# Attention and GeGLU on one core: the order of two exps in shared steps, and the planner's table of engine times

## The chip, the core and the metric

The kernel runs on one NeuronCore of a Trainium2 chip. The metric is device time in microseconds (us) of one execution; each kernel is run several times and the median counts. The profile shows one execution, taken by the hardware profiler. Four engines matter here: TensorE (PE in the profile, with its weight loads as PEld), ScalarE (ACT), VectorE (DVE) and GpSimd (POOL). SyncE (SP) only issues DMAs.

## The reference

A pre-norm transformer block over 2048 tokens of width 640, with 32 query heads of width 20 that share one key and one value head, and a GeGLU feed-forward layer of width 1536. Everything is bfloat16 outside the accumulations. Cut to its core:

```
xn = (x - mean(x)) / sqrt(var(x) + 1e-5)
q = xn @ wq  -> 32 heads x 20;   k = xn @ wk;   v = xn @ wv        # one k, one v
p = softmax(q k^T / sqrt(20))                                       # 32 x 2048 x 2048
h = x + concat(p v) @ wo
hn = layernorm(h)
out = h + (gelu(hn @ w_gate) * (hn @ w_up)) @ w_down                # gelu in its tanh form
```

The softmax needs 32 x 2048 x 2048 = 134 million exponentials, which is where most of the time goes.

## The kernel before

**Tiling.** The 2048 tokens are 16 tiles of 128 (NT). For each tile of queries the heads are taken in two halves, and for each half the 16 tiles of keys are gone through one after the other. One such combination is a *step*; there are NS = 512 of them, 32 to a tile. A step computes four scores matmuls (L729) that use four row strips of the PE array at once, each a 128x512 block: 128 keys by 4 heads x 128 queries. Each fills one bank of the scores memory (PSUM).

**Banks.** Of the eight banks six form three pairs (A_BANKS, pool pA). A step takes two pairs, `t1` and `t2`. So the next step finds one pair left over from the step before this one, and has to wait until this step gives back its first pair. One more bank collects the weighted sum of values (V_BANKS), one serves all projections (M_BANKS).

**The exps.** In a plain step ACT takes the exp of both pairs, each in one instruction over 1024 columns (`exp2`, L745, tile `pa_sb`): a *pair exp*. In a *shared* step ACT does one pair exp and, of the other pair, one bank (`exp1`, L754, tile `ps_sb`): a *half-bank exp*. The second bank of that pair is done by DVE with integer arithmetic on the bits of a bfloat16 (`exp_dve`): `e1` (L768, tile `ej`) reads the bank and so frees it, and for each two such banks four more instructions over 1024 columns finish the exp: `e2` (L779, tile `eu`), `e3` (L781, tile `et`), `e4` (L782, tile `et`), `e5` (L783, tile `pd_sb`). The pair is given back when both the half-bank exp and e1 have read it (`t2.n_rel = 2`).

**The rest.** Four matmuls per step multiply the exps with the values (PV, L840, `v_ext`). Every 16 steps the sums are evacuated, their reciprocals taken through a small trip to HBM and back, and multiplied in on POOL. Every 32 steps a tile goes through the output projection (L917), a layer norm on DVE, a transposing DMA, and the feed-forward matmuls (L992, L1031), which are cut into chunks and laid between the steps of later tiles; so are the query projections (L632). DVE evacuates their results.

**What sets the order.** A planner in the kernel, run while the program is built, writes out the order of each engine's queue. It simulates the five engines with a table of times: each `Op` has a duration on its engine, and `SEEN[engine]` is added before a result counts as visible to the one that waits for it. An engine takes, among the operations that can start first, the one of lowest `prio`; exps and e1 have -1000. `urgent` keeps PE from beginning a chunk that would hold up the next scores matmuls. Whether a step is shared is decided when its scores have been placed (`scored`): it is, if the work that DVE still has to do adds up to less than `D_BACKLOG` = 800 ns. Each engine gets its queue in the order written, with waits on semaphores where an input comes from elsewhere.

Of the kernel before, what the change touches and what calls it, by code (L numbers as in the profile page):

```python
# [8 lines left out]
ALU = mybir.AluOpType  # L9
# [8 lines left out]
SEEN = {"pe": 120.0, "act": 60.0, "dve": 50.0, "pool": 60.0, "sp": 0.0}  # L18
DRAIN = 107.0
SP_ISSUE = 550.0  # L20

# [43 lines left out]
class Planner:  # L65
# [107 lines left out]
    def run(self):  # L173
        while True:
            best = None
            for e in ENGINES:
# [21 lines left out]
                if best is None or first < best[0]:  # L198
                    if e == "pe":
                        u = self.urgent(first)  # L200
                        if u is not None:
                            ok = [(a, op) for a, op in tl if op.prio <= -1000 or
                                  a + op.dur + (DRAIN if op.mode != self.pe_mode else 0.0) <= u or a >= u]
                            if not ok:
                                continue
                            tl = ok
                            first = min(a for a, _ in tl)
                            if best is not None and first >= best[0]:
                                continue
                    pick = min((op.prio, a, k) for k, (a, op) in enumerate(tl) if a <= first + 1e-6)  # L210
                    best = (first, e, tl[pick[2]][1])
# [103 lines left out]
def bass_sequential_preLN__grouped_kv_mqa__glu_gated_geglu__prompt_kernel(  # L315
# [26 lines left out]
    D_FROM, D_BACKLOG, SLACK = 14, 800.0, 100.0  # L342
    MLAG, DLAG, VLAG, VLATE = 300.0, 100.0, 400.0, 1200.0
# [106 lines left out]
    def dve(fn, n, deps, prio, mode=1.04, fix=150.0, **kw):  # L450
        return op("dve", fn, fix + n * mode, deps, prio, **kw)
# [8 lines left out]
    def evac(eng, o_ap, i_ap, n, deps, prio, **kw):  # L460
        return op(eng, copy_fn(o_ap, i_ap), (220 + .833 * n) if eng == "act" else (150 + 1.04 * n), deps, prio, **kw)
# [47 lines left out]
    def ln(which, t0, n, src, prio, gate=None, free=None, tmode="dma"):  # L509
# [3 lines left out]
        for t in range(t0, t0 + n):  # L513
            for hf in range(2):
                st.append(dve((lambda t, hf: lambda e: e.bn_stats(
                    stats[:, L, t, 6 * hf:6 * hf + 6], xh[:, t, hf * hq:(hf + 1) * hq]))(t, hf),
                    hq, (src(t),), prio, fix=130, gate=gate, name=f"st{L}.{t}"))
        ag = []
        for t in range(t0, t0 + n):
            ag.append(dve((lambda t: lambda e: e.bn_aggr(mv[:, L, t, :], stats[:, L, t, :]))(t), 12,  # L520
                          st[2 * (t - t0):2 * (t - t0) + 2], prio, fix=195, name=f"ag{L}.{t}"))
        a = dve(lambda e: e.tensor_copy(mvb[:, L, sl, :], mv[:, L, sl, :]), 2 * n, ag, prio, fix=165)
        b = dve(lambda e: e.tensor_copy(mvf[:, L, sl, :], mvb[:, L, sl, :]), 2 * n, (a,), prio, fix=165)
        c = dve(lambda e: e.tensor_scalar_add(veb[:, L, sl], mvf[:, L, sl, 1], EPS), n, (b,), prio, fix=170)
        d = op("pool", lambda e: e.tensor_tensor(den[:, L, sl], veb[:, L, sl], halfc[:, 0:n], ALU.pow),
               230 + 170 * n, (c, m_half), prio - 50)
        r = dve(lambda e: e.reciprocal(rsd[:, L, sl], den[:, L, sl]), n, (d,), prio, fix=175)
        res = []
        for t in range(t0, t0 + n):
# [3 lines left out]
                D, (r, b, src(t)), prio, mode=.26, fix=220, acq=[tl], name=f"nm{L}.{t}")  # L533
# [226 lines left out]
    def exp_dve(o_, tile):  # L760


        if dstate["tile"] is None:
# [6 lines left out]
            690, (o_,), prio=-1000, acq=[jt] if k == 0 else [], name="e1"))  # L770
        pl.rel(tile, p1)
        firsts.append(p1)
        if k == 0:
            fin = Op("dve", None, 690, (), prio=-950, acq=[pt], name="e5", late=VLATE)
            dstate["fin"] = fin
        fin = dstate["fin"]
        if k == 1:
            ut, wt = Tile(pU), Tile(pW)
            e2 = pl.add(Op("dve", lambda e: e.tensor_scalar(eu[:], ej[:, jt.slot, :], 127, None, ALU.bitwise_and),  # L779
                           430, firsts, prio=-950, acq=[ut], name="e2"))  # L780
            e3 = pl.add(Op("dve", lambda e: e.tensor_scalar(et[:], eu[:], C2, C1, ALU.mult, ALU.add), 430, (e2,), prio=-950, acq=[wt], name="e3"))  # L781
            e4 = pl.add(Op("dve", lambda e: e.tensor_tensor(et[:], et[:], eu[:], ALU.mult), 690, (e3, e2), prio=-950, name="e4"))  # L782
# [20 lines left out]
    def scored(s, o_, t1, t2):  # L803
# [144 lines left out]
    def ln2(t, r1, r2, prio):  # L948
# [3 lines left out]
        s0 = dve(lambda e: e.bn_stats(stats[:, L, t, 0:6], xh[:, t, 0:hq]), hq, (r1,), p, fix=130)  # L952
        s1 = dve(lambda e: e.bn_stats(stats[:, L, t, 6:12], xh[:, t, hq:D]), hq, (r1, r2), p, fix=130)
        ag = dve(lambda e: e.bn_aggr(mv[:, L, t, :], stats[:, L, t, :]), 12, (s0, s1), p, fix=195)
        a = dve(lambda e: e.tensor_copy(mvb[:, L, sl, :], mv[:, L, sl, :]), 2, (ag,), p, fix=165)
        b = dve(lambda e: e.tensor_copy(mvf[:, L, sl, :], mvb[:, L, sl, :]), 2, (a,), p, fix=165)
        c = dve(lambda e: e.tensor_scalar_add(veb[:, L, sl], mvf[:, L, sl, 1], EPS), 1, (b,), p, fix=170)
        d = op("pool", lambda e: e.tensor_tensor(den[:, L, sl], veb[:, L, sl], halfc[:, 0:1], ALU.pow),
               400, (c, m_half), p - 50)
        r = dve(lambda e: e.reciprocal(rsd[:, L, sl], den[:, L, sl]), 1, (d,), p, fix=175)  # L960
# [3 lines left out]
            D, (r, b, r1, r2), p, mode=.26, fix=220, acq=[tl])  # L964
# [164 lines left out]
```

## Time and profile before

| | |
|---|---|
| median of 3 runs | 1015.47 us (1013.6 to 1015.71) |
| profiled execution | 1015.34 us, of it span of the instructions 1013.6 us |
| ACT busy | 887.5 us (88%) |
| DVE busy | 735.9 us (73%) |
| PE busy | 705.4 us (70%) |
| mean granted clock of PE | 0.853 |
| first pair exp to last pair exp | about 20 us to 981 us |
| pair exps, half-bank exps | 708, 316 |

Busy time is the sum of what the profile shows as the duration of instructions. Instructions of one engine can overlap at their ends, so three pair exps in a row take less than three durations; the distance from start to start is what the engine's queue goes by. A row of the timeline merges equal neighbours: "x3" is three instructions, and the time beside it runs from the start of the first to the end of the last. The number in brackets is how long the engine was idle before, and what ended that. PEclk is the share of its full clock that PE was granted; the records have it at 1.00 or 0.50, and means lie between.

### The profile page before, as it was taken

The numbers are of one execution on the slowest core, as the hardware profiler recorded it, in microseconds if no ns is written. First come the engines' busy times: TensorE is split into PE (matmuls) and PEld (weight loads), VectorE is DVE, ScalarE is ACT, GpSimd is POOL, SyncE is SP. The second block draws the span as 40 slices with busy tenths as digits, with TensorE's granted clock in tenths as the row PEclk, the third lists the DMA queues.
The fourth block names the chain that finished last, engine by engine and source line by source line (L and its number), as shares of the span: only waits on it lengthen the run. The fifth ranks groups of instructions, "written<-read, shape, count | busy, mean of one in ns | idle before, by whom it ended". The sixth has DMA issues, their size and how long they took to land.

```text
span 1013.6 us, 15962 instructions
## 1 busy us (share of the span) xinstructions
PE 705.4 (70%) x6313; PEld 276.9 (27%) x6313; DVE 735.9 (73%) x1447; ACT 887.5 (88%) x1056; POOL 66.9 (7%) x70
## 2 busy tenths in 40 slices
PE   2665756777777667667677676767777676777687
PEld 2321111232223222233222331223222222212245
DVE  8457677787878777876787676876788766778654
ACT  2698888899899999999999998999989999989971
POOL 5000000010001000000000000000000000000000
PEclk9776665798789998998898987988979888869899
DMA  6750000000000000000000000000000000000010
GB/s 171 124 209 12 12 18 12 8 22 8 12 25 19 12 18 16 17 12 12 19 25 18 4 16 12 25 19 12 15 11 18 18 12 19 19 14 20 7 22 21
DMA packets 47282, 27.42 MB, mean 27 GB/s; under 512 B 34408, under 2 KB 41960, under 8 KB 47208
## 3 DMA queue, kind: packets, MB, share of 16 engines
q1 hardware_dynamic: 47208, 26.40, 10.3%
q8 instruction: 50, 0.82, 0.3%
q14 instruction: 24, 0.20, 0.1%
HBM read 18.34 MB, written 2.88 MB: 21 GB/s over the span
## 4 chain that ended last, share of the span: by engine, by line
ACT 53%; PE 28%; DVE 11%; issue 5%; DMA 2%; POOL 0%; SPq 0%; POOLq 0%
ACT pa_sb L745 47%; PE ps L729 14%; PE ps L992 5%; DVE ej L768 4%; PE ps L840 4%; ACT ps_sb L754 3%; PE ps L1031 2%; ACT gh L1010 2%; PE ps L632 2%; DVE eu L779 1%; DVE et L781 1%; PE ps L917 1%; DMA xnT<-xn 1%; ACT L745 1%; ACT L1010 1%
## 5 line engine op out<-in xcount | busy, mean ns | idle before, releaser
L745 ACT ACTIVATE pa_sb<-ps 128x1024 bf16<-128x1024 f32 x708 | 685.5, 1032 | 83.5 <-PE ps L729 66.3
L729 PE MATMUL ps<-qT,kT 32*128 32x512 bf16 x2048 | 233.7, 443 | 265.9 <-ACT pa_sb L745 212.8
L768 DVE TENSOR_SCALAR ej<-ps 128x512 uint16<-128x512 f32 x316 | 218.1, 690 | 174.2 <-PE ps L729 172.4
L754 ACT ACTIVATE ps_sb<-ps 128x512 bf16<-128x512 f32 x316 | 190.3, 602 | 0.8 <-PE ps L729 0.8
L729 PEld LDWEIGHTS ps<-qT,kT 32*128 32x128 bf16 x2048 | 59.9, 93 | 473.4 <-ACT pa_sb L745 201.4
L840 PE MATMUL ps<-pa_sb,v_ext 128*32 128x512 bf16 x1416 | 176.6, 436 | 4.2 <-ACT pa_sb L745 3.3
L840 PE MATMUL ps<-ps_sb,v_ext 128*32 128x512 bf16 x316 | 116.3, 443 | 0.0
L840 PE MATMUL ps<-pd_sb,v_ext 128*32 128x512 bf16 x316 | 116.3, 443 | 0.0
L782 DVE TENSOR_TENSOR et<-et,eu 128x1024 bf16<-128x1024 bf16 x158 | 111.2, 704 | 2.2
L783 DVE TENSOR_TENSOR pd_sb<-ej,et 128x1024 uint16<-128x1024 uint16 x158 | 107.9, 683 | 0.9
L890 POOL TENSOR_TENSOR onT<-osb,rL 128x512 bf16<-128x512 f32 x31 | 40.5, 1305 | 628.3 <-DMA rL<-lscr 628.3
L992 PE MATMUL ps<-xnT,wu 128*128 128x256 bf16 (+1 forms) x540 | 74.8, 286 | 8.2 <-ACT gh L1010 8.2
L1031 PE MATMUL ps<-wd,gh 128*128 128x128 bf16 (+1 forms) x384 | 74.3, 326 | 1.4 <-DVE gh L1015 0.7
L781 DVE TENSOR_SCALAR et<-eu 128x1024 bf16<-128x1024 uint16 x158 | 72.4, 458 | 2.3
L992 PE MATMUL ps<-xnT,wg 128*128 128x256 bf16 (+1 forms) x540 | 72.0, 276 | 0.4 <-DVE gh L457 0.4
L779 DVE TENSOR_SCALAR eu<-ej 128x1024 uint16<-128x1024 uint16 x158 | 67.8, 429 | 2.3
L840 PEld LDWEIGHTS ps<-pa_sb,v_ext 128*32 128x32 bf16 x1416 | 41.0, 100 | 88.8 <-issue 55.7
L992 PEld LDWEIGHTS ps<-xnT,wu 128*128 128x128 bf16 x540 | 46.2, 104 | 35.4 <-issue 16.0
L917 PE MATMUL ps<-wo_pad,onT 128*128 128x512 bf16 (+1 forms) x256 | 50.8, 330 | 2.6 <-DVE onT L874 1.1
L992 PEld LDWEIGHTS ps<-xnT,wg 128*128 128x128 bf16 x540 | 45.2, 102 | 25.3 <-issue 14.2
L1015 DVE TENSOR_TENSOR gh<-gh,ps 128x512 bf16<-128x512 bf16 x48 | 32.8, 686 | 20.9 <-PE ps L992 20.4
L632 PE MATMUL ps<-xnT,wq_pad 128*128 128x256 bf16 x280 | 47.3, 309 | 0.0
(68 smaller groups left out, 416.8 us busy)
## 6 DMA issues: line engine op xcount, KB each, us to landing
rL<-lscr SPq DMA_DIRECT2D x124, 64.0 KB, 2.0
out_dram<-xh SPq DMA_DIRECT2D x16, 160.0 KB, 1.8
lcol<-osb SPq DMA_DIRECT2D x124, 2.0 KB, 1.7
xh<-in_A_x_dram SPq DMA_DIRECT2D x6, 320.0 KB, 6.8
wg<-in_B_w_gate_dram SPq DMA_DIRECT2D x1, 1920.0 KB, 8.2
wu<-in_B_w_up_dram SPq DMA_DIRECT2D x1, 1920.0 KB, 12.5
wd<-in_B_w_down_dram SPq DMA_DIRECT2D x1, 1920.0 KB, 17.3
gh<-in_A_wq_dram SPq DMA_DIRECT2D x2, 400.0 KB, 4.6
```

The lines of the kernel that those rows point to most:

```text
L632: ins = e.matmul(tbank(mt)[:, i * 256:(i + 1) * 256], wq_pad[:, c, g, :], xnT[:, c, tok], start=(c == 0), stop=(c == ND - 1))
L729: ins = e.matmul(bank(A_BANKS[(t1, t1, t2, t2)[r].slot] + r % 2), kT4[32 * r:32 * r + 32, kt * P:(kt + 1) * P], qT[32 * r:32 * r + 32, (t ...
L745: ex = pl.add(Op("act", lambda e: e.activation(pa_sb[:, pt.slot, :], bank(A_BANKS[tile.slot], 2), ACT.Exp, scale=SM), 928, (o_,), prio=-10 ...
L754: ex = pl.add(Op("act", lambda e: e.activation(ps_sb[:, pt.slot, :], bank(A_BANKS[tile.slot]), ACT.Exp, scale=SM), 502, (o_,), prio=-1000, ...
L768: p1 = pl.add(Op("dve", lambda e: e.tensor_scalar(ej[:, jt.slot, k * 512:(k + 1) * 512], bank(A_BANKS[tile.slot] + 1), EA, EB, ALU.mult, A ...
L779: e2 = pl.add(Op("dve", lambda e: e.tensor_scalar(eu[:], ej[:, jt.slot, :], 127, None, ALU.bitwise_and), 430, firsts, prio=-950, acq=[ut], ...
L781: e3 = pl.add(Op("dve", lambda e: e.tensor_scalar(et[:], eu[:], C2, C1, ALU.mult, ALU.add), 430, (e2,), prio=-950, acq=[wt], name="e3"))
L782: e4 = pl.add(Op("dve", lambda e: e.tensor_tensor(et[:], et[:], eu[:], ALU.mult), 690, (e3, e2), prio=-950, name="e4"))
L783: fin.fn = lambda e: e.tensor_tensor(pd_sb[:, pt.slot, :], ej[:, jt.slot, :], et[:], ALU.add)
L840: ins = e.matmul(bank(V_BANKS[vt.slot])[32 * r:32 * r + 32, :], v_ext[:, kt, :], us[r][2](), start=(kt == 0), stop=(kt == NKT - 1), tile_p ...
L992: ins = e.matmul(tbank(m)[:, j * n:(j + 1) * n], w[:, c, fc * P:(fc + 1) * P], xnT[:, c, tok], start=(c == 0), stop=(c == ND - 1))
L1031: ins = e.matmul(tbank(tl_)[:, 0:c1 - c0], H(f // nfu, f // nfu + 1)[:, (f % nfu) * n + i * P:(f % nfu) * n + (i + 1) * P], wd[:, f, c0:c1 ...
```

## The change

It has three parts.

1. In a shared step the pair that ACT and DVE share can now be `t1`, with its half-bank exp (and e1) first and the pair exp second. That is done when DVE, by the plan, is free no later than 150 ns (`D_EARLY`) after the scores are seen; else the order is as before.
2. The planner's table of times is split in two: an operation's duration is now the distance after which its engine can start the next one, and the rest until a result is seen is in `SEEN` (by another engine) and `SELF` (by the same engine). Durations of DVE instructions fall, most of them by 70 to 90 ns, `SEEN` rises from 60 to 220 ns for ACT and from 50 to 190 ns for DVE.
3. DVE may be kept free: if an e1 can start within 300 ns (`HOLD`), only operations that end before it are placed ahead of it.

```diff
-SEEN = {"pe": 120.0, "act": 60.0, "dve": 50.0, "pool": 60.0, "sp": 0.0}
+SEEN = {"pe": 120.0, "act": 220.0, "dve": 190.0, "pool": 150.0, "sp": 0.0}
+SELF = {"pe": 0.0, "act": 150.0, "dve": 115.0, "pool": 80.0, "sp": 0.0}
+HOLD = 300.0
...
         if d.eng == op.eng:
-            return d.end + SEEN[d.eng]
+            return d.end + SELF[d.eng]
...
-                    pick = min((op.prio, a, k) for k, (a, op) in enumerate(tl) if a <= first + 1e-6)
-                    best = (first, e, tl[pick[2]][1])
+                    lim = first + 1e-6
+                    if e == "dve":
+                        soon = [a for a, op in tl if op.prio <= -1000 and a <= first + HOLD]
+                        if soon:
+                            lim = min(soon) + 1e-6
+                            tl = [(a, op) for a, op in tl if a > first + 1e-6 or op.prio <= -1000 or a + op.dur <= lim]
+                            lim = max(lim if all(a > first + 1e-6 for a, op in tl if op.prio > -1000) else first + 1e-6, min(a for a, _ in tl))
+                    pick = min((op.prio, a, k) for k, (a, op) in enumerate(tl) if a <= lim)
+                    best = (max(first, tl[pick[2]][0]), e, tl[pick[2]][1])
...
-    def dve(fn, n, deps, prio, mode=1.04, fix=150.0, **kw):
+    def dve(fn, n, deps, prio, mode=1.04, fix=72.0, **kw):
...
             ej[:, jt.slot, k * 512:(k + 1) * 512], bank(A_BANKS[tile.slot] + 1), EA, EB, ALU.mult, ALU.add),
-            690, (o_,), prio=-1000, acq=[jt] if k == 0 else [], name="e1"))
+            610, (o_,), prio=-1000, acq=[jt] if k == 0 else [], name="e1"))
...
-        us = exp2(o_, t1)
         use_d = dstate["tile"] is not None or (D_FROM <= s < NS - 6 and dve_backlog(o_.end) < D_BACKLOG)
         if use_d:
-            t2.n_rel = 2
-            us.append(exp1(o_, t2))
-            us.append(exp_dve(o_, t2))
-            state["nd"] = state.get("nd", 0) + 1
+            first = pl.free["dve"] < o_.end + SEEN["pe"] + D_EARLY
+            ta, td = (t2, t1) if first else (t1, t2)
+            td.n_rel = 2
+            if first:
+                us = [exp1(o_, td), exp_dve(o_, td)]
+                us += exp2(o_, ta)
+            else:
+                us = exp2(o_, ta)
+                us += [exp1(o_, td), exp_dve(o_, td)]
         else:
-            us += exp2(o_, t2)
+            us = exp2(o_, t1) + exp2(o_, t2)
```

The other lines of the diff are durations of the same kind (e2 and e3 from 430 to 345, e4 and e5 from 690 to 610, and the small instructions of the layer norms).

**What it does to the queues.** In the program that is built, 334 of 340 shared steps have the half-bank exp first. There were 316 shared steps; there are now 340, so 684 pair exps in place of 708, and 12 more groups e1, e1, e2 to e5 on DVE. Two places show how the queues changed. The rows give line, instruction, tiles, size, and the semaphore waited for (s_pe is PE's, s_dve DVE's own).

ACT's queue in the first tile, a few shared steps after sharing begins. Before:

```order
L754 ACTIVATE ps_sb<-ps 128x512
L745 ACTIVATE pa_sb<-ps 128x1024 [waits s_pe]
L754 ACTIVATE ps_sb<-ps 128x512
L745 ACTIVATE pa_sb<-ps 128x1024 [waits s_pe]
L754 ACTIVATE ps_sb<-ps 128x512
L745 ACTIVATE pa_sb<-ps 128x1024 [waits s_pe]
L745 ACTIVATE pa_sb<-ps 128x1024
```

Now:

```order
L756 ACTIVATE pa_sb<-ps 128x1024
L765 ACTIVATE ps_sb<-ps 128x512 [waits s_pe]
L756 ACTIVATE pa_sb<-ps 128x1024
L765 ACTIVATE ps_sb<-ps 128x512 [waits s_pe]
L756 ACTIVATE pa_sb<-ps 128x1024
L756 ACTIVATE pa_sb<-ps 128x1024 [waits s_pe]
L756 ACTIVATE pa_sb<-ps 128x1024
```

The wait for the step's scores has moved from the pair exp to the half-bank exp: instructions still alternate, but a shared step now begins with the short one and ends with the long one.

DVE's queue at the first four shared steps (`ej` is e1, `eu` e2, `et<-eu` e3, `et<-et,eu` e4, `pd_sb` e5, `qT` the evacuation of a query projection). Before:

```order
L768 TENSOR_SCALAR ej<-ps 128x512 [waits s_pe]
L457 CAST qT<-ps 128x512 [waits s_pe]
L768 TENSOR_SCALAR ej<-ps 128x512 [waits s_pe]
L782 TENSOR_TENSOR et<-et,eu 128x1024 [waits s_dve]
L779 TENSOR_SCALAR eu<-ej 128x1024 [waits s_dve]
L783 TENSOR_TENSOR pd_sb<-ej,et 128x1024
L768 TENSOR_SCALAR ej<-ps 128x512 [waits s_dve,s_pe]
```

Now:

```order
L779 TENSOR_SCALAR ej<-ps 128x512 [waits s_pe]
L468 CAST qT<-ps 128x512 [waits s_pe]
L779 TENSOR_SCALAR ej<-ps 128x512 [waits s_pe]
L793 TENSOR_TENSOR et<-et,eu 128x1024
L794 TENSOR_TENSOR pd_sb<-ej,et 128x1024 [waits s_dve]
L790 TENSOR_SCALAR eu<-ej 128x1024
L792 TENSOR_SCALAR et<-eu 128x1024 [waits s_dve]
L793 TENSOR_TENSOR et<-et,eu 128x1024 [waits s_dve]
L779 TENSOR_SCALAR ej<-ps 128x512 [waits s_pe]
```

Between the fourth and the fifth e1 stand now five instructions in place of three: e5 of the first group directly after its e4, and most of the second group.

More of the change, by code (lines that the diff above doesn't have):

```diff
@@ L342, in bass_sequential_preLN__grouped_kv_mqa__glu_gated_geglu__prompt_kernel @@
     D_FROM, D_BACKLOG, SLACK = 14, 800.0, 100.0
+    D_EARLY = 150.0
     MLAG, DLAG, VLAG, VLATE = 300.0, 100.0, 400.0, 1200.0
@@ L516, in ln @@
                     stats[:, L, t, 6 * hf:6 * hf + 6], xh[:, t, hf * hq:(hf + 1) * hq]))(t, hf),
-                    hq, (src(t),), prio, fix=130, gate=gate, name=f"st{L}.{t}"))
+                    hq, (src(t),), prio, fix=60, gate=gate, name=f"st{L}.{t}"))
         ag = []
@@ L773, in exp_dve @@
         if k == 0:
-            fin = Op("dve", None, 690, (), prio=-950, acq=[pt], name="e5", late=VLATE)
+            fin = Op("dve", None, 610, (), prio=-950, acq=[pt], name="e5", late=VLATE)
             dstate["fin"] = fin
@@ L779, in exp_dve @@
             e2 = pl.add(Op("dve", lambda e: e.tensor_scalar(eu[:], ej[:, jt.slot, :], 127, None, ALU.bitwise_and),
-                           430, firsts, prio=-950, acq=[ut], name="e2"))
-            e3 = pl.add(Op("dve", lambda e: e.tensor_scalar(et[:], eu[:], C2, C1, ALU.mult, ALU.add), 430, (e2,), prio=-950, acq=[wt], name="e3"))
-            e4 = pl.add(Op("dve", lambda e: e.tensor_tensor(et[:], et[:], eu[:], ALU.mult), 690, (e3, e2), prio=-950, name="e4"))
+                           345, firsts, prio=-950, acq=[ut], name="e2"))
+            e3 = pl.add(Op("dve", lambda e: e.tensor_scalar(et[:], eu[:], C2, C1, ALU.mult, ALU.add), 345, (e2,), prio=-950, acq=[wt], name="e3"))
+            e4 = pl.add(Op("dve", lambda e: e.tensor_tensor(et[:], et[:], eu[:], ALU.mult), 610, (e3, e2), prio=-950, name="e4"))
             fin.fn = lambda e: e.tensor_tensor(pd_sb[:, pt.slot, :], ej[:, jt.slot, :], et[:], ALU.add)
@@ L963, in ln2 @@
             xn[:, tl.slot, :], xh[:, t, :], mvf[:, L, t, 0:1], rsd[:, L, t:t + 1], ALU.subtract, ALU.mult),
-            D, (r, b, r1, r2), p, mode=.26, fix=220, acq=[tl])
+            D, (r, b, r1, r2), p, mode=.26, fix=190, acq=[tl])
         return [(nm, tl)]
```

28 lines of the change are left out of this document (14 added, 14 removed).

## The prediction

> **What bounds the kernel now.** The page comes first: its shares and its costliest groups.
>
> ```profile
> span 1013.6 us, 15962 instructions
> PE 705.4 (70%) x6313; PEld 276.9 (27%) x6313; DVE 735.9 (73%) x1447; ACT 887.5 (88%) x1056; POOL 66.9 (7%) x70
> ...
> ACT 53%; PE 28%; DVE 11%; issue 5%; DMA 2%; POOL 0%; SPq 0%; POOLq 0%
> ...
> L745 ACT ACTIVATE pa_sb<-ps 128x1024 bf16<-128x1024 f32 x708 | 685.5, 1032 | 83.5 <-PE ps L729 66.3
> ...
> L768 DVE TENSOR_SCALAR ej<-ps 128x512 uint16<-128x512 f32 x316 | 218.1, 690 | 174.2 <-PE ps L729 172.4
> L754 ACT ACTIVATE ps_sb<-ps 128x512 bf16<-128x512 f32 x316 | 190.3, 602 | 0.8 <-PE ps L729 0.8
> ```
>
> ACT is the busiest engine, and it idles before pair exps, waiting for scores (PE, L729). The half-bank exps hardly wait: each follows a pair exp of its own step. So the stall falls once per step, before the pair exp that opens it. To see its size I went to the timeline, first where PE had its full clock (508.3 to 528.7 us, row further down):
>
> ```profile
> 508.93 2.85 ACT L745 ACTIVATE pa_sb<-ps 128x1024 bf16<-128x1024 f32 x3 [0.60 <-PE ps L729]
> ...
> 512.28 1.02 ACT L745 ACTIVATE pa_sb<-ps 128x1024 bf16<-128x1024 f32 x1
> 512.28 0.69 DVE L768 TENSOR_SCALAR ej<-ps 128x512 uint16<-128x512 f32 x1 [0.44 <-PE ps L729]
> 513.21 0.59 ACT L754 ACTIVATE ps_sb<-ps 128x512 bf16<-128x512 f32 x1
> 513.45 0.40 PE L729 MATMUL ps<-qT,kT 32*128 32x512 bf16 x4 [0.68 <-ACT pa_sb L745]
> 513.90 2.85 ACT L745 ACTIVATE pa_sb<-ps 128x1024 bf16<-128x1024 f32 x3
> ...
> 524.06 1.02 ACT L745 ACTIVATE pa_sb<-ps 128x1024 bf16<-128x1024 f32 x1
> 525.67 1.02 ACT L745 ACTIVATE pa_sb<-ps 128x1024 bf16<-128x1024 f32 x1
> 527.28 1.02 ACT L745 ACTIVATE pa_sb<-ps 128x1024 bf16<-128x1024 f32 x1
> 528.89 1.94 ACT L745 ACTIVATE pa_sb<-ps 128x1024 bf16<-128x1024 f32 x2
> ```
>
> Read it as a loop. The pair exp runs 512.28 to 513.30; only then is a bank pair free, and the next scores start at 513.45 (0.15 later), take 0.40, and the next exp starts at 513.90 (0.05 later). 1.02 + 0.15 + 0.40 + 0.05 = 1.62 us, which is the distance 512.28 to 513.90. The next shared steps take 1.61 each (524.06, 525.67, 527.28, 528.89). ACT itself needs less: three pair exps in 2.85 us start (2.85 - 1.02) / 2 = 0.915 apart, so 0.10 of an exp's duration lies under the next; a half-bank exp then takes 0.602 - 0.11 = 0.49. Together 1.41. A shared step loses 0.20 us, because the short exp does not cover the scores.
>
> The same at half clock:
>
> ```profile
> 502.62 1.02 ACT L745 ACTIVATE pa_sb<-ps 128x1024 bf16<-128x1024 f32 x1 [0.23 <-PE ps L729]
> 503.79 0.62 PE L729 MATMUL ps<-qT,kT 32*128 32x512 bf16 x4 [0.25 <-ACT pa_sb L745]
> 504.33 1.89 PE L1031 MATMUL ps<-wd,gh 128*128 128x512 bf16 x4
> 504.45 1.02 ACT L745 ACTIVATE pa_sb<-ps 128x1024 bf16<-128x1024 f32 x1 [0.32 <-PE ps L729]
> 506.82 1.02 ACT L745 ACTIVATE pa_sb<-ps 128x1024 bf16<-128x1024 f32 x1 [0.86 <-PE ps L729]
> 506.82 0.69 DVE L768 TENSOR_SCALAR ej<-ps 128x512 uint16<-128x512 f32 x1 [1.34 <-PE ps L729]
> ```
>
> The scores take 0.62 and the loop is 1.83. The step from 504.45 takes 2.37: there PE is held by four matmuls of the feed-forward layer (1.89 us), which no order of exps changes.
>
> How many steps are of which kind comes from the windows view for L754 (columns: stretch, length, busy with count, PEclk), and four stretches of all engines:
>
> ```profile
> 52.00:201.00 149.00, 32.26 (x54) 0.66 0.13 42
> 201.00:960.00 759.00, 156.20 (x259) 0.88 0.06 16
> ...
> 498.00:508.20 10.20, 7.23 (x42) 1.47 (x42) 8.34 (x14) 8.47 (x12) 1.05 (x1) 0.50 0.01 2
> 508.30:528.70 20.40, 14.67 (x150) 5.14 (x146) 16.83 (x31) 19.37 (x25) 1.27 (x1) 1.00 0.07 23
> ...
> 617.60:627.70 10.10, 7.13 (x42) 1.48 (x42) 7.30 (x13) 8.37 (x12) 0.09 (x1) 0.50 0.01 2
> 627.80:648.00 20.20, 14.47 (x153) 5.05 (x146) 16.69 (x30) 19.23 (x25) 1.39 (x1) 1.00 0.10 23
> ```
>
> A mean clock c between 0.5 and 1 means a share of 2 x (1 - c) at half clock: 68% of the first stretch, 24% of the second. So 0.68 x 54 + 0.24 x 259 = 99 shared steps ran at half clock, 217 at full clock.
>
> **The change part by part.** *Half-bank exp first.* The next scores now wait for the half-bank exp (0.60) and e1 (0.69), both started by the same scores. The trace has no scores released by an e1 alone; the nearest row is the 0.15 behind the pair exp, and I take it. From e1's start: 0.69 + 0.15 + 0.40 + 0.05 = 1.29 us to the next exp at full clock. Meanwhile ACT is busy for 0.49 + 0.915 = 1.41 us, so the scores are hidden and ACT sets the pace, with 0.12 to spare. At half clock the loop is 0.69 + 0.15 + 0.62 + 0.05 = 1.51, still 0.10 over ACT's time. The price that the trace does not show is how late e1 starts: below zero it can't go; from above, it can stand behind one DVE instruction of 0.69 that has just started. In the rows above e1 starts with the pair exp (512.28, 506.82). I add 0.02: 1.43 and 1.52.
>
> At full clock, 1.60 now (1.62, 1.61, 1.61, 1.61 above, and the step before 512.28, which is 508.93 + 2 x 0.915 = 510.76 to 512.28, 1.52): 217 x (1.60 - 1.43) = 37 us. The bounds are 217 x 0.19 = 41 us and, with each e1 a whole instruction late, a loss (below). At half clock I take three steps in four as free of a blocking chunk: the steps of 616.81 to 626.42 below take 1.84, 1.74 (from 618.65 + 2 x 0.915 = 620.48), 1.83 and 2.37. The three average 1.80: 74 x (1.80 - 1.52) = 21 us. The bounds are zero (PE blocked anyway) and 99 x 0.31 = 31.
>
> ```profile
> 616.81 1.02 ACT L745 ACTIVATE pa_sb<-ps 128x1024 bf16<-128x1024 f32 x1
> 618.65 2.86 ACT L745 ACTIVATE pa_sb<-ps 128x1024 bf16<-128x1024 f32 x3 [0.32 <-PE ps L729]
> 622.22 1.02 ACT L745 ACTIVATE pa_sb<-ps 128x1024 bf16<-128x1024 f32 x1 [0.23 <-PE ps L729]
> 624.05 1.02 ACT L745 ACTIVATE pa_sb<-ps 128x1024 bf16<-128x1024 f32 x1 [0.32 <-PE ps L729]
> 626.42 1.02 ACT L745 ACTIVATE pa_sb<-ps 128x1024 bf16<-128x1024 f32 x1 [0.86 <-PE ps L729]
> ```
>
> *More sharing.* 24 steps of two pair exps (2 x 0.915 = 1.83) become shared ones: 24 x (1.83 - 1.43) = 10 us. Bounds: 0 if DVE can't keep up, and 24 x 0.42 = 10.
>
> *DVE.* Twelve more groups cost two e1 and the four rows below: 2 x 0.690 + 0.429 + 0.458 + 0.704 + 0.683 = 3.65 us each, 44 us.
>
> ```profile
> L782 DVE TENSOR_TENSOR et<-et,eu 128x1024 bf16<-128x1024 bf16 x158 | 111.2, 704 | 2.2
> L783 DVE TENSOR_TENSOR pd_sb<-ej,et 128x1024 uint16<-128x1024 uint16 x158 | 107.9, 683 | 0.9
> ...
> L781 DVE TENSOR_SCALAR et<-eu 128x1024 bf16<-128x1024 uint16 x158 | 72.4, 458 | 2.3
> ...
> L779 DVE TENSOR_SCALAR eu<-ej 128x1024 uint16<-128x1024 uint16 x158 | 67.8, 429 | 2.3
> ```
>
> 735.9 + 44 = 780 us in a span of some 945 is 83% (73% before). I cost it at nothing: its cover is the remaining idle time, some 165 us. If that cover goes, the price is a late e1, which is rival 2.
>
> *The planner's table.* By itself it moves work and removes none. Its numbers come close to this trace (e1 690 ns long by its row; two pair exps start 915 apart, planned with 928), so I cost it at nothing: chunks of PE are still placed between scores. *Waits moved.* Behind ACT's wait, now at the half-bank exp, stands only the pair exp of the same scores. On DVE e2 to e5 of the group before queue behind a waiting e1; PV of that step waits for e5, and PE's later scores stand behind PV. Start (to 20 us) and tail (from 981 us) keep their instructions but for a few feed-forward matmuls that move out of the tail: zero, give or take 3.
>
> Sum: 37 + 21 + 10 = 68. The profiled execution took 1015.34 us (span 1013.6 and 1.7 around it), 0.13 under the median of the runs: 1015.34 - 68 = **947 us**.
>
> **The rivals.** *1. PE's clock rises.* In the rows above half clock goes with few matmuls (42 in 10.2 and 10.1 us), full clock with many (150 in 20.4, 153 in 20.2). Steps that follow each other faster give PE more to do per microsecond. If half clock ended, the 74 free steps would gain 0.09 each (7 us), and 25 blocked ones, 2.37 now, would come to 1.43 (23 us): 947 - 30 = 917. Against it: the chunks lie as unevenly as before. [...]
>
> *2. DVE is often late.* If in half of the shared steps an e1 starts 0.30 late (half an instruction), these take 1.59 at full clock and 1.81 at half clock: means 1.51 and 1.66. Gain: 217 x 0.09 + 74 x 0.14 + 24 x 0.32 = 38 us, so 977. For it: DVE at 83%, and now on the releasing chain of every shared step, with 0.12 to spare. Against it: e1 is planned first, and DVE is held free for it.
>
> *3. Slower: the DVE queue stalls the scores.* e1 now releases each next step, so one mechanism can cost all: an e1 stuck in order behind an instruction that itself waits (e5's group, a projection not yet done). It decides from a mean lateness of 0.31 (1.29 + 0.31 = 1.60, today's step). At 0.40: 1.69 at full clock, 217 x 0.09 = 20; at half clock 1.91, 74 x 0.11 = 8; less sharing's rest, 24 x 0.14 = 3: 1015 + 25 = 1040. For it: the 1.34 us of DVE idling at 506.82, with other work queued behind that e1. Against it: that wait was for PE, not the reverse. [...]
>
> *4. Nothing moves.* Half-bank first is planned for 334 of 340 steps, so the order does change; only a new bound at today's pace would give about 1015. PE is not it (705.4 of 947 is 74%).
>
> **How the numbers follow.** Forecast 50% (its own range 927 to 964), clock 17%, late DVE 22%, slower 7%, nothing 4%. Two in ten lie outside 910 to 983: part of rival 1 below, rivals 3 and 4 and the worse part of rival 2 above. A measurement of this kernel tells about 0.2% (2 us) from no change. Faster: 50 + 17 + 22 + 1 of rival 4 = 90%; same 2%; slower 7 + 1 = 8%.
>
> **What would show it.** Right: shared steps open with the half-bank exp, about 1.43 us from one to the next at full clock; ACT's idle time before L745 shrinks from 83.5 to under 30 us, and what is left moves before the half-bank exps; ACT at 90% or more; DVE near 83%, with e1 starting within 0.1 us of the half-bank exp. Late DVE would show as scores whose last releaser is e1, over 1.29 us after the step's start. A clock above 0.90 speaks for rival 1. The forecast is wrong if shared steps at full clock stay above 1.55 us, or if plain steps, 1.83 now, grow.

## The result, and the profile after

The changed kernel takes 945.8 us (median of 3 runs, 942.1 to 946.8), against 1015.47 before: a ratio of 0.931, 95% interval 0.9267 to 0.9353. The forecast was 947 us. The profiled execution took 946.8 us, its span 945.0.

The page of the kernel after, the lines that answer to those quoted before:

```profile
span 945.0 us, 16050 instructions
PE 689.0 (73%) x6280; PEld 271.4 (29%) x6313; DVE 769.4 (81%) x1519; ACT 852.8 (90%) x1056; POOL 69.0 (7%) x70
...
ACT 61%; PE 20%; DVE 15%; DMA 2%; issue 1%; SPq 0%; POOL 0%; DVEq 0%
...
L756 ACT ACTIVATE pa_sb<-ps 128x1024 bf16<-128x1024 f32 x684 | 698.5, 1118 | 25.0 <-PE ps L740 23.4
...
L779 DVE TENSOR_SCALAR ej<-ps 128x512 uint16<-128x512 f32 x340 | 234.0, 688 | 113.1 <-PE ps L740 108.9
L765 ACT ACTIVATE ps_sb<-ps 128x512 bf16<-128x512 f32 x340 | 232.1, 683 | 28.9 <-PE ps L740 28.2
```

ACT's idle time before pair exps fell from 83.5 to 25.0 us; 28.9 us now stand before the half-bank exps, which open the shared steps. On the chain of waits PE's share fell from 28 to 20%. The timeline of the kernel after, at full clock, shows the new loop (start, duration, engine, line):

```profile
483.99 0.40 PE L740 MATMUL ps<-qT,kT 32*128 32x512 bf16 x4 [0.16 <-ACT ps_sb L765]
...
484.44 0.69 DVE L779 TENSOR_SCALAR ej<-ps 128x512 uint16<-128x512 f32 x1
...
484.65 0.63 ACT L765 ACTIVATE ps_sb<-ps 128x512 bf16<-128x512 f32 x1
...
485.12 1.07 ACT L756 ACTIVATE pa_sb<-ps 128x1024 bf16<-128x1024 f32 x1
...
485.33 0.39 PE L740 MATMUL ps<-qT,kT 32*128 32x512 bf16 x4
...
485.78 0.69 DVE L779 TENSOR_SCALAR ej<-ps 128x512 uint16<-128x512 f32 x1
...
486.03 0.66 ACT L765 ACTIVATE ps_sb<-ps 128x512 bf16<-128x512 f32 x1
```

From one half-bank exp to the next it is 486.03 - 484.65 = 1.38 us, and ACT does not wait: the scores that start at 485.33 are done at 485.72, 0.31 before ACT takes them. e1 takes them first (485.78). The scores now run a little ahead of ACT, where before ACT stood waiting for them.

This run-ahead is not always there. In 92 places (waits view further down) the scores wait for an e1, as here at full clock, where ACT had waited and e1 started 0.12 late:

```profile
523.20 0.60 ACT L765 ACTIVATE ps_sb<-ps 128x512 bf16<-128x512 f32 x1 [0.49 <-PE ps L740]
523.32 0.69 DVE L779 TENSOR_SCALAR ej<-ps 128x512 uint16<-128x512 f32 x1
...
524.15 0.40 PE L740 MATMUL ps<-qT,kT 32*128 32x512 bf16 x4 [0.35 <-DVE ej L779]
...
524.60 0.61 ACT L765 ACTIVATE ps_sb<-ps 128x512 bf16<-128x512 f32 x1
```

From e1's start it is 0.69 + 0.14 + 0.40 + 0.05 = 1.28 us to the next half-bank exp, and 1.40 us from one half-bank exp to the next.

At half clock a feed-forward chunk still gets in the way. The same view, some steps earlier:

```profile
476.38 0.61 PE L740 MATMUL ps<-qT,kT 32*128 32x512 bf16 x4
...
476.93 2.62 PE L1046 MATMUL ps<-wd,gh 128*128 128x512 bf16 x6
...
477.05 1.94 ACT L756 ACTIVATE pa_sb<-ps 128x1024 bf16<-128x1024 f32 x2 [1.40 <-PE ps L740]
...
479.48 0.40 PE L740 MATMUL ps<-qT,kT 32*128 32x512 bf16 x4
...
479.81 0.60 PE L1046 MATMUL ps<-wd,gh 128*128 128x512 bf16 x2
...
479.92 1.94 ACT L756 ACTIVATE pa_sb<-ps 128x1024 bf16<-128x1024 f32 x2 [0.94 <-PE ps L740]
```

**A ledger of the steps.** From the start times of all exps I took the distance from each step's first exp to the next step's, and sorted the steps by the granted clock at their start; the first 20 steps, the last 6, and steps over 3 us are left out. Of these long steps seven have a gelu in them, before and after; another one before and two after were held up by matmuls laid between the scores.

| | before: steps, mean us, sum | after: steps, mean us, sum |
|---|---|---|
| shared, full clock | 211, 1.604, 338.5 | 252, 1.434, 361.5 |
| shared, half clock | 97, 1.936, 187.8 | 82, 1.83, 150.1 |
| plain, full clock | 130, 1.819, 236.4 | 115, 1.819, 209.2 |
| plain, half clock | 39, 1.99, 77.7 | 28, 2.07, 57.9 |

Together 840.4 before (and one odd step of 2.0) against 778.7: 64 us. The rest of the 68.6 us between the spans lies in the steps left out, in a first exp that comes 1.4 us later (21.7 against 20.3 us) and in a tail after the last pair exp starts that is 3.6 us shorter (30.0 against 33.6 us).

### The profile page after: what moved, and what is told of

The parts are those of the page before. It is cut to its first block, busy times and chain, and to the rows that moved or that the text cites. A ratio compares the mean times of both kernels' runs of the same rounds, so it can differ in the third digit from the quotient of the medians.

```text
span 945.0 us, 16050 instructions
## 1 busy us (share of the span) xinstructions
PE 689.0 (73%) x6280; PEld 271.4 (29%) x6313; DVE 769.4 (81%) x1519; ACT 852.8 (90%) x1056; POOL 69.0 (7%) x70
## 4 chain that ended last, share of the span: by engine, by line
ACT 61%; PE 20%; DVE 15%; DMA 2%; issue 1%; SPq 0%; POOL 0%; DVEq 0%
ACT pa_sb L756 46%; ACT ps_sb L765 12%; PE ps L740 6%; DVE ej L779 4%; PE ps L855 4%; PE ps L1007 4%; PE ps L1046 2%; DVE et L793 2%; ACT gh L1025 2%; PE ps L932 1%; PE ps L643 1%; DVE pd_sb L794 1%; DVE et L792 1%; DVE stats L526 1%; DVE eu L790 1%
## 5 line engine op out<-in xcount | busy, mean ns | idle before, releaser
L756 ACT ACTIVATE pa_sb<-ps 128x1024 bf16<-128x1024 f32 x684 | 698.5, 1118 | 25.0 <-PE ps L740 23.4
L779 DVE TENSOR_SCALAR ej<-ps 128x512 uint16<-128x512 f32 x340 | 234.0, 688 | 113.1 <-PE ps L740 108.9
L765 ACT ACTIVATE ps_sb<-ps 128x512 bf16<-128x512 f32 x340 | 232.1, 683 | 28.9 <-PE ps L740 28.2
L855 PE MATMUL ps<-ps_sb,v_ext 128*32 128x512 bf16 x340 | 123.3, 436 | 3.2 <-DVE pd_sb L794 2.4
L793 DVE TENSOR_TENSOR et<-et,eu 128x1024 bf16<-128x1024 bf16 x170 | 120.7, 710 | 2.9
L794 DVE TENSOR_TENSOR pd_sb<-ej,et 128x1024 uint16<-128x1024 uint16 x170 | 119.7, 704 | 3.2
L790 DVE TENSOR_SCALAR eu<-ej 128x1024 uint16<-128x1024 uint16 x170 | 75.2, 442 | 0.7
L1046 PE MATMUL ps<-wd,gh 128*128 128x128 bf16 (+1 forms) x367 | 65.7, 311 | 6.3 <-issue 2.8
L932 PE MATMUL ps<-wo_pad,onT 128*128 128x128 bf16 (+1 forms) x240 | 48.5, 331 | 15.2 <-POOL onT L905 8.8
L855 PEld LDWEIGHTS ps<-ps_sb,v_ext 128*32 128x32 bf16 x340 | 21.5, 97 | 59.1 <-issue 48.4
```

Source lines behind the costliest of these rows:

```text
L756: ex = pl.add(Op("act", lambda e: e.activation(pa_sb[:, pt.slot, :], bank(A_BANKS[tile.slot], 2), ACT.Exp, scale=SM), 928, (o_,), prio=-10 ...
L765: ex = pl.add(Op("act", lambda e: e.activation(ps_sb[:, pt.slot, :], bank(A_BANKS[tile.slot]), ACT.Exp, scale=SM), 502, (o_,), prio=-1000, ...
L779: p1 = pl.add(Op("dve", lambda e: e.tensor_scalar(ej[:, jt.slot, k * 512:(k + 1) * 512], bank(A_BANKS[tile.slot] + 1), EA, EB, ALU.mult, A ...
L794: fin.fn = lambda e: e.tensor_tensor(pd_sb[:, pt.slot, :], ej[:, jt.slot, :], et[:], ALU.add)
L855: ins = e.matmul(bank(V_BANKS[vt.slot])[32 * r:32 * r + 32, :], v_ext[:, kt, :], us[r][2](), start=(kt == 0), stop=(kt == NKT - 1), tile_p ...
L932: ins = e.matmul(tbank(tl_)[:, 0:c1 - c0], onT[:, nt_.slot, g, :], wo_pad[:, g, c0:c1], start=(g == 0), stop=(g == NG - 1))
```

## The experiments

Twelve runs, each beside the kernel before on the same chip (1014.8 to 1014.9 us there); the changed kernel is the result above, with 1015.47 us beside it, so kernels of different rows are best compared by their ratios. Times are medians. Clock and half-clock time, 2 x (1 - mean clock) x span, are those of the profiled execution; executions of one program differ in both (no_hold: 959.0 us at 0.875 in the profiled one, 966.1 at 0.858 in another).

| run | shared steps | us | ratio to before, 95% | mean clock | half-clock us |
|---|---|---|---|---|---|
| changed kernel | 340 | 945.8 | 0.931, 0.927 to 0.935 | 0.870 | 246 |
| pair_first | 370 | 1004.2 | 0.989, 0.987 to 0.991 | 0.855 | 290 |
| order_alone | 326 | 955.6 | 0.941, 0.940 to 0.943 | 0.889 | 212 |
| no_hold | 384 | 963.4 | 0.949, 0.946 to 0.952 | 0.875 | 239 |
| share_318 | 318 | 941.5 | 0.928, 0.926 to 0.929 | 0.891 | 205 |
| order_hold | 302 | 976.1 | 0.962, 0.961 to 0.964 | 0.858 | 277 |
| scores_twice | 340 | 973.1 | 0.959, 0.957 to 0.961 | 0.939 | 119 |
| scores_twice_318 | 318 | 986.5 | 0.973, 0.971 to 0.974 | 0.933 | 132 |
| scores_half_more_318 | 318 | 959.1 | 0.945, 0.942 to 0.947 | 0.907 | 178 |
| no_hold_340 | 340 | 943.1 | 0.927, 0.923 to 0.932 | 0.895 | 198 |
| hold100_322 | 322 | 945.8 | 0.931, 0.928 to 0.934 | 0.875 | 236 |
| hold200_326 | 326 | 956.0 | 0.941, 0.938 to 0.945 | 0.877 | 235 |
| hold200_316 | 316 | 962.0 | 0.946, 0.943 to 0.950 | 0.870 | 250 |

### Which part carries the gain

**pair_first** undoes the order and keeps everything else:

```diff
-            first = pl.free["dve"] < o_.end + SEEN["pe"] + D_EARLY
+            first = False
```

> The changed kernel with one part undone: shared steps always take the pair exp first, as before. The planner's new table and the keeping free of DVE stay; the plan then has 370 shared steps, all pair exp first. Theory A (the order of the two exps carries the gain): the loop is back at about 1.60 us at full clock and 1.80 at half clock, so about 1000 us (1015 less 54 more shared steps x 0.23, some 12 us); the idle time of ACT before pair exps is back at 80 us or more. Rival B (the planner's new table carries it, since queues planned with true latencies wait less): below 965 us. Both in equal parts: about 980 us.

Measured 1004.2 us. Theory A holds. The stall is back where it was (page of this run):

```profile
L756 ACT ACTIVATE pa_sb<-ps 128x1024 bf16<-128x1024 f32 x654 | 640.4, 1028 | 90.1 <-PE ps L740 72.7
...
L765 ACT ACTIVATE ps_sb<-ps 128x512 bf16<-128x512 f32 x370 | 221.7, 599 | 0.0
```

Shared steps at full clock take 1.600 us in the mean, as before the change. The new table, the keeping free of DVE and 54 more shared steps together bring 10.6 us, where the additional sharing alone was priced at 12.

**order_alone** is the kernel before, with the order swapped in every shared step:

```diff
-        us = exp2(o_, t1)
...
-            t2.n_rel = 2
-            us.append(exp1(o_, t2))
-            us.append(exp_dve(o_, t2))
...
+            t1.n_rel = 2
+            us = [exp1(o_, t1), exp_dve(o_, t1)]
+            us += exp2(o_, t2)
...
```

> The kernel before with one part of the change alone: in shared steps the half-bank exp and e1 come first and the pair exp second, always. The planner's old table stays, and DVE is not kept free; 326 shared steps. Theory A (the order carries it): shared steps near 1.43 us at full clock, 1015 less 37 (full clock), 21 (half clock) and 10 x 0.40 (more sharing), about 953 us. Rival B (the table carries it): 1005 us or more. Rival C (the order needs an e1 that is on time, and the old table, with its DVE instructions 80 ns too long and latencies too short, does not plan for it): e1 late by 0.1 to 0.4 us in many steps, 965 to 990 us.

Measured 955.6 us, 59 of the 70 us. Theory A holds again; shared steps at full clock take 1.457 us, with the old table, which has an e1's result seen 50 ns after its end where the rows at 524.15 show 0.14 us. The page of this run:

```profile
L745 ACT ACTIVATE pa_sb<-ps 128x1024 bf16<-128x1024 f32 x698 | 702.2, 1098 | 24.6 <-PE ps L729 20.6
...
L768 DVE TENSOR_SCALAR ej<-ps 128x512 uint16<-128x512 f32 x326 | 224.6, 689 | 113.4 <-PE ps L729 108.8
L754 ACT ACTIVATE ps_sb<-ps 128x512 bf16<-128x512 f32 x326 | 217.0, 666 | 30.0 <-PE ps L729 29.5
```

The idle time before pair exps is as low as in the whole change.

### What keeping DVE free is worth

**order_hold** adds the keeping free of DVE to order_alone (the same lines as in the change), with the old table:

> The kernel before with two of the three parts: half-bank exp first in every shared step, and DVE kept free up to 300 ns for an e1, but with the old table of times; 302 shared steps. Order alone took 955.6 us, the whole change 945.8. Theory A (keeping DVE free is what brings the other 10 us, by punctual e1s): 940 to 950 us, shared steps at full clock at 1.43 us or less. Rival B (it needs the new table, since a DVE that is believed to be 80 ns slower per instruction is kept idle for too long and shares fewer steps): 955 us or more, by 24 fewer shared steps and no shorter ones.

Measured 976.1 us, 20 us more than without it. Rival B holds in direction, but the price is larger than its 24 fewer shared steps (24 x 0.41 = 10 us), and the steps did get shorter: the keeping free does what it is for, and shared steps at full clock fall from 1.457 to 1.410 us. Against it stand fewer shared steps and 277 us at half clock in place of 212. Neighbouring plans differ by as much as these 20 us (below), so one plan does not give the price of keeping DVE free.

**no_hold** takes it out of the changed kernel:

```diff
-HOLD = 300.0
+HOLD = -1.0
```

> The changed kernel without the keeping free of DVE for an e1 that is due within 300 ns. The plan then has 384 shared steps, 373 of them half-bank exp first (changed kernel: 340 and 334). Theory A (keeping DVE free is what makes e1 punctual): e1 starts up to one DVE instruction late in a good part of the steps, shared steps at full clock at 1.50 us or more; 384 x 0.08 = 31 us lost against 44 x 0.40 = 18 won, about 958 us. Rival B (e1 is punctual anyhow, since it comes first among what can start): 44 more shared steps x 0.40, about 928 us.

Measured 963.4 us, which fits theory A's figures: shared steps at full clock take 1.514 us, a quarter of them over 1.54. In half of them (139 of 272) e1 starts more than 0.10 us after the half-bank exp, and these take 1.61 us in the mean, the others 1.41. In the changed kernel e1 is that late in 51 of 252. But two things had changed, the keeping free and the number of shared steps, so **no_hold_340** sets the limit on waiting work to 500 ns, which gives 340 shared steps again:

```diff
-HOLD = 300.0
+HOLD = -1.0
...
-    D_FROM, D_BACKLOG, SLACK = 14, 800.0, 100.0
+    D_FROM, D_BACKLOG, SLACK = 14, 500.0, 100.0
```

> The changed kernel without the keeping free of DVE, and with the limit on work waiting for DVE lowered (500 in place of 800 ns) so that exactly as many steps are shared as in the changed kernel, 340 (337 half-bank exp first). So the keeping free is the difference, at equal sharing. Theory A (it is worth what punctual e1s bring, and the 963 us of the run without it were not due to the 384 shared steps): 955 us or more, shared steps at full clock at 1.48 us or more (changed kernel: 1.43). Rival B (the slow run came from sharing 384 steps on a DVE busy for 831 us): within 4 us of the changed kernel's 945.8, shared steps at 1.43 to 1.45.

Measured 943.1 us: rival B holds in the time, though its pace of 1.43 to 1.45 us is missed. At equal sharing the whole is not slower without keeping DVE free. Its pace at full clock is slower (1.461 us against 1.434, with e1 late in 91 of 261 steps; scores waited for e1 for 77.5 us, in the waits view below, against 52.7 in the changed kernel), some 260 x 0.03 = 7 us, but it spent 198 us at half clock in place of 246. So late e1s come from both, the missing reserve and the 384 shared steps, and the loss in no_hold came with the plan that shares 384. The limit on waiting work differs too, so the two kernels are two plans and not one plan with one thing taken out.

```profile
PE ps L740 <- DVE ej L779: 77.5, 106, 2.0
PE ps L740 <- ACT pa_sb L756: 76.5, 115, 1.4
```

The same view of the changed kernel:

```profile
PE ps L740 <- ACT pa_sb L756: 70.4, 104, 1.9
...
PE ps L740 <- DVE ej L779: 52.7, 92, 1.5
```

### What more sharing is worth

**share_318** lowers `D_BACKLOG` from 800 to 600 ns and nothing else:

> The changed kernel with a lower limit on the work waiting for DVE (600 in place of 800 ns), so that 318 steps are shared in place of 340, nearly as many as before the change (316); all but one have the half-bank exp first. Theory A (more sharing was worth 10 us of the gain, 0.40 a step): 22 x 0.40 = 9 us slower than the changed kernel, about 955 us. Rival B (sharing is paid for with a busier DVE and late e1s, and is worth nothing): 946 us or less.

Measured 941.5 us, with an interval that overlaps the changed kernel's. Theory A falls, rival B's number holds: no slower with 22 fewer shared steps, where I had priced them at 9 us. Shared steps at full clock are hardly shorter (1.421 us); half-clock time is 205 us in place of 246. Whether this is a price of sharing or luck in how the chunks fell, the next runs were to tell; they do not settle it.

**scores_twice** issues the four scores matmuls of each step twice, and **scores_twice_318** does the same on share_318:

```diff
-            for r in range(4):
+            for r in (0, 1, 2, 3, 0, 1, 2, 3):
                 ins = e.matmul(
                     bank(A_BANKS[(t1, t1, t2, t2)[r].slot] + r % 2), ...
```

> The changed kernel with the four scores matmuls of each step issued twice (the same result, written twice): PE gets 2048 more matmuls and nothing else changes. It asks whether the half clock comes from a PE that has too little to do, and how much room the scores have. Theory A (clock follows PE's load; the scores end 0.25 us before ACT needs them at full clock, and 0.21 more fits): mean clock 0.95 or more, and the 106 steps that now run at half clock (78 shared at 1.83, 28 plain at 2.07) fall to 1.43 and 1.82, 38 us less: about 908 to 918 us. Rival B (the clock does not follow the load): about 0.87 still, each step at half clock 0.43 longer, 46 us more: 990 us. Rival C (the clock rises, but the room is the 0.12 us that the prediction worked out): 250 x 0.09 = 22 us back, about 930 us.

> The same doubling of the scores matmuls, on the kernel with 318 shared steps (941.5 us). It asks why sharing 22 more steps did not pay. Theory A (more sharing costs where PE runs at half clock, since the feed-forward chunks then block scores for longer; with a full clock 22 shared steps win 0.40 each): with the clock up, this one is 5 to 9 us slower than the same doubling at 340 shared steps. Rival B (it is DVE, busier by 44 us, that makes up for it at any clock): equal to it within 3 us, or faster.

Measured 973.1 and 986.5 us. The clock does follow PE's load: from 0.870 to 0.939 and from 0.891 to 0.933, and half-clock time falls from 246 to 119 us and from 205 to 132. But the additional work did not fit, so the time is worse; theory A's time falls, and rival C had the right mechanism but too small a price: it put it at 22 us, while 298 shared steps at full clock went from 1.434 to 1.578 us, 43 us, and the run is 27 us slower even with the clock's gain. The timeline of scores_twice at full clock, one loop:

```profile
475.77 0.60 ACT L765 ACTIVATE ps_sb<-ps 128x512 bf16<-128x512 f32 x1
475.78 0.69 DVE L779 TENSOR_SCALAR ej<-ps 128x512 uint16<-128x512 f32 x1 [0.21 <-PE ps L740]
...
476.27 1.02 ACT L756 ACTIVATE pa_sb<-ps 128x1024 bf16<-128x1024 f32 x1
...
476.61 0.61 PE L740 MATMUL ps<-qT,kT 32*128 32x512 bf16 x8
...
477.27 0.60 ACT L765 ACTIVATE ps_sb<-ps 128x512 bf16<-128x512 f32 x1
```

e1 ends at 476.47, the scores start 0.14 later, take 0.61, and the next exp starts 0.05 after them: 0.69 + 0.14 + 0.61 + 0.05 = 1.49 of the 1.50 us from 475.77 to 477.27. This is the loop of the prediction, with longer scores. It also shows that the 0.25 us I had read as room in the changed kernel is a run-ahead, which builds up over steps (in the changed kernel e1 starts 0, 0.12, 0.21 and 0.25 us ahead of the half-bank exps at 481.87, 483.27, 484.65 and 486.03) while the loop (1.29) is shorter than ACT's time (1.38); the room per step is the difference, 0.09. Of the additional 0.21 us per step 0.12 are then left over, and by that much the median shared step at full clock grew (1.38 to 1.50).

As to sharing: with nearly equal clocks, 340 shared steps beat 318 by 13.5 us (expected 5 to 9). Theory A holds in direction, but not all of this is sharing. By the step times of the two traces, 20 more plain steps (1.88 us in the mean, against 1.62 for shared ones) make 5 us. The plan with 318 also has twelve steps over 3 us (68.2 us) in place of eight (54.4), which makes some 7, and a tail 2 us longer. So these two runs fit the priced worth of sharing; they do not show it alone. In the kernels as they stand the 22 steps came with 41 us more at half clock.

**scores_half_more_318**, also on share_318, repeats only half the columns:

```diff
+            for r in range(4):
+                e.matmul(bank(...)[:, 0:256], kT4[...], qT[..., 4 * hf:4 * hf + 2, ...], start=True, stop=True, ...)
```

> As the run before, but the additional scores matmuls have half the columns (256 of 512, ahead of the full ones, which overwrite them): half the additional work for PE. Theory A (clock follows load, by a limit): mean clock between 0.89 (none) and that of the full doubling, near 0.95; about 925 us. Rival B (no effect on the clock): 0.89 and 89 x 0.21 = 19 us slower, 960 us.

Measured 959.1 us and a clock of 0.907, between none (0.891) and twice (0.933). The clock rises step by step with the load, as in theory A. Its time of 925 us is missed: the run is 17.6 us slower than share_318. The time is near rival B's 960, whose reason, no effect on the clock, is refuted.

### Plans near the changed kernel

Three more plans, with DVE kept free for other lengths and other limits on waiting work (`HOLD`, `D_BACKLOG`: 100 and 500, 200 and 600, 200 and 400):

> The changed kernel with DVE kept free up to 100 ns (in place of 300) and a limit of 500 ns on work waiting for it: 322 shared steps, 320 half-bank exp first. A look for a faster balance near the 318 shared steps that took 941.5 us. Theory A (sharing less, not the length of the keeping free, is what made that run faster): 939 to 944 us. Rival B (300 ns is needed for punctual e1s): 950 us or more.

> As the run before, with 200 ns and a limit of 600 ns: 326 shared steps, 322 half-bank exp first. Theory A: 939 to 945 us. Rival B (the time follows the time that PE spends at half clock, which a plan hits or misses by chance of where its chunks fall): anything from 935 to 960 us, in the order of the half-clock times (mean clock under 0.875: over 945).

> As the run before, with 200 ns and a limit of 400 ns: 316 shared steps, all half-bank exp first; as many as the kernel before the change had. Theory A (the order alone at equal sharing brings the whole gain): 938 to 945 us. Rival B (half-clock time decides among plans so near to each other): 935 to 960 us, in the order of the mean clocks.

Measured 945.8, 956.0 and 962.0 us. Theory A falls: with 316 to 326 shared steps the times spread over 16 us. Rival B's order by clock doesn't hold either: 0.875, 0.877 and 0.870, and the changed kernel has 0.870 at 945.8. Plans with all three parts of the change that differ only in these two numbers lie between 941 and 962 us. What decides among them stays open; the number of shared steps, the mean clock and the pace at full clock (1.42, 1.45 and 1.44 us here) each explain a part of it at best. Another part are steps without a gelu that still take 3.0 to 3.4 us; the three plans have two, five and six of them. At the sharing of the kernel before (316) the last plan is still 53 us faster than that kernel, which again is the order. No plan that was tried beats the changed kernel by more than the intervals allow.

## Why the prediction was right

**The loop.** Right. The price of the order at full clock was 217 steps from 1.60 to 1.43 us, 37 us; measured are 211 steps from 1.604 to a mean of 1.434, 36 us. Both experiments that separate the order from the rest (1004 with everything else, 956 with the order alone) give it the bulk of the gain. The time after e1, taken as 0.15 us from the pair exp's row, is 0.14 in the rows at 524.15, and 0.147 in the median of all scores that waited for an e1. ACT's own time per step was put at 1.41 and is 1.38. The allowance for a late e1 was 0.02; the mean step lies 0.05 over ACT's time, two thirds of it in 51 steps whose e1 starts more than 0.10 us late (1.56 us in the mean, the other 201 take 1.40). That the two errors cancel to 1.43 is luck.

**Half clock.** The mechanism was right, the size too large. Forecast was 1.80 to 1.52 us for the free steps; the median of the half-clock shared steps went from 1.83 to 1.54. But the blocked ones got longer (nine in ten were under 2.37 us before, under 2.70 after), so the mean fell only from 1.94 to 1.83; the rows at 476.93 show such a blocking chunk, at a plain step. The ledger: 97 such steps took 187.8 us; now 82 take 150.1, and the other 15 at full clock 15 x 1.434 = 21.5. That is 16 us where 21 were forecast, and 15 steps of it come from rival 1.

**More sharing.** The ledger shows what was priced: 26 plain steps fewer, each 1.86 in the mean of before, at 1.434: 11 us for 10. But a kernel with nearly the old sharing (share_318) is just as fast, so as a cause this term is not confirmed for the kernel as it is. The runs with doubled scores fit it, with the reservation made there.

**The planner's table at nothing.** Right with the pair exp first: there table, keeping free and more sharing made 10.6 us together, no more than the sharing was priced at. On top of the order it is not shown. The two other parts made 955.6 into 945.8, and order and table without keeping DVE free (no_hold_340) made it 943.1, with 14 more shared steps, worth some 6 us at 0.40 each. So keeping DVE free is not needed for these 10 us, and the table may be worth a few. But neighbouring plans spread over more than that, and order and table alone with 326 shared steps were not run, so the split stays open.

**DVE** is busy for 769.4 us, 81% (forecast 780 and 83%). e1 is on time for the most part: in the changed kernel's full-clock steps half of them start within 0.12 us before to 0.05 after the half-bank exp, but one in five starts more than 0.10 after it, and fewer than half lie within 0.1 us of it, which the prediction had named as a sign. Rival 2 shows in no_hold, where 384 shared steps took DVE to 831 us, half of the e1s came late and the shared steps took 1.51, the value worked out for it. Rival 3 was not seen. **Rival 1** came true in part: the mean clock rose from 0.853 to 0.870, and half-clock time fell from 298 to 246 us, not to nothing. **Start and tail** moved by +1.4 and -3.6 us, about the 3 allowed.

**The sum.** Forecast were 37 + 21 + 10 = 68 us; the ledger has 36 + 16 + 11 = 63, and start, tail and the steps left out bring the rest. That the total came out within 2 us is in part luck; that the order brings most of it is not.

## What to carry to other kernels

When a queue alternates long and short instructions, and a buffer is given back by the first one, put the short one first: what has to be refilled then hides under the long one (here shared steps at full clock went from 1.60 to 1.43 us). Write such a loop out as the sum of its links (0.69 + 0.15 + 0.40 + 0.05) beside the busy engine's own time per step; the larger of the two was the pace here in three different kernels, before (1.62), after (1.38) and with doubled scores (1.50), in shared steps at full clock that no other matmuls held up. And treat a few per cent between neighbouring plans of an automatic planner with care: here they spread over 20 us without any one cause that I could show.

## What I had not expected of the hardware

**The duration of an ACT instruction in the profile depends on what stands before it.** Pair exps read 1032 ns before the change and 1118 after, half-bank exps 602 and 683, though neither changed, and ACT's distance from start to start did not grow: from a pair exp on it is mostly 0.904 us now and was 0.904 or 0.920 before, and 0.477 from a half-bank exp to the pair exp behind it, where nothing waits. The timeline of ACT in the kernel after shows the records grow over a stretch without a wait:

```profile
482.37 1.02 ACT L756 ACTIVATE pa_sb<-ps 128x1024 bf16<-128x1024 f32 x1
...
489.69 1.15 ACT L756 ACTIVATE pa_sb<-ps 128x1024 bf16<-128x1024 f32 x1
...
498.84 1.30 ACT L756 ACTIVATE pa_sb<-ps 128x1024 bf16<-128x1024 f32 x1
```

In scores_twice, where ACT waits for scores before 128 of the 340 half-bank exps (57 in the changed kernel), the page reads

```profile
L756 ACT ACTIVATE pa_sb<-ps 128x1024 bf16<-128x1024 f32 x684 | 676.8, 1026 | 25.0 <-PE ps L740 23.1
...
L765 ACT ACTIVATE ps_sb<-ps 128x512 bf16<-128x512 f32 x340 | 204.4, 601 | 33.5 <-PE ps L740 29.3
```

Over the whole trace of the kernel after, pair exps directly behind a wait read 1.02 us in the mean, and those with 30 or more ACT instructions since the last wait 1.19. What the longer records consist of stays open. They do not add up to the busy time: 684 x 1.118 + 340 x 0.683 = 997 us is more than the span. The page's busy time is the time in which at least one instruction of the engine was in flight, and not the sum of their durations. The distance between starts is the measure of ACT's work: 684 x 0.904 + 340 x 0.477 = 781 us of exps.

**PE's clock rose with its load, and a gelu was not enough to lose it.** Where ACT changes tables, takes a gelu and changes back, no exps are made for 5.3 us, and here PE falls to half clock at 438.3, 2.6 us after they begin again. The timeline of ACT in the kernel after, and then its windows around that place (stretch, length, busy time of PE, PEld, DVE, ACT and POOL, PEclk, DMA share, GB/s):

```profile
430.35 1.28 ACT L1025 ACT_TABLE_LOAD   x1
431.64 2.76 ACT L1025 ACTIVATE gh<-gh 128x3072 bf16<-128x3072 bf16 x1
434.41 1.28 ACT L756 ACT_TABLE_LOAD   x1
```

```profile
407.60:438.30 30.70, 21.95 (x223) 9.53 (x216) 24.40 (x43) 30.38 (x36) 2.51 (x2) 1.00 0.04 10
438.30:448.50 10.20, 9.22 (x55) 3.08 (x54) 8.10 (x20) 8.98 (x13) 0.00 (x0) 0.50 0.00 0
448.60:469.10 20.50, 14.40 (x150) 6.43 (x148) 19.45 (x38) 20.50 (x27) 1.08 (x2) 1.00 0.10 23
469.10:479.30 10.20, 8.06 (x47) 1.89 (x48) 8.74 (x15) 7.65 (x10) 1.17 (x1) 0.50 0.01 2
```

That load raises the clock is shown by the doubled scores, 0.870 to 0.939. A gelu is neither needed nor enough for half clock. The stretch from 469.10 has none ahead of it: the last ended at 434.41, and 20.5 us at full clock lie between. In the changed kernel half clock begins within 8 us of each of the seven gelus between the steps, but in no_hold_340 two of seven, at 650.8 and 758.9 us, are followed by 24 us or more at full clock, and in the changed kernel the one in the tail, at 918.87 us, by full clock to the end of the span, 24.6 us. Whether a gelu makes half clock likelier was not tested. In the trace of the changed kernel the half-clock stretches last from 3.41 to 37.55 us, all of them whole multiples of 3.41 (10.24 each for the two above); what sets these lengths was not tested.
